# Moving a small MLP's VectorE work from between the key chunks to the ends of the key pairs, and looping its unrolled code, in a decode attention kernel

## The chip, the cores and the metric

The kernel runs on one core of one Trainium2 chip. The metric is the device time of a run in microseconds (us). A profile (one traced run) stands beside the timed runs. All traced runs were fast, and the comparisons use fast runs alone.

## The reference, cut to what matters

A decode step: one query token, 16 query heads over 8 key/value heads, a cache of 65,536 positions of 256 numbers for each. To its output a gated "mixer", a tiny MLP over the token axis, is added.

```python
q = (x @ wq) ...                                   # 16 heads of 256
scores = einsum("bhqd,bhkd->bhqk", q, k) * 256**-0.5
o = einsum("bhqk,bhkd->bhqd", softmax(scores), v)
a = o.reshape(...) @ wo
# the mixer: x is one row of 448; F = 1792 = 14 tiles of 128
h = layernorm(x);  u = gelu(einsum("bsd,sf->bdf", h, w1) + b1)
b = einsum("bdf,fs->bds", u, w2) + b2
out = g * a + (1 - g) * b                          # g: a sigmoid gate
```

The cache is 2 x 8 x 65,536 x 256 bf16 numbers, 537 MB. Each is used once, for two query heads.

## The kernel before

The cache is streamed in "pairs": 16,384 positions of K in two halves of 4 MB, then the same positions of V in one load of 8 MB. There are 32 pairs, four for each head. A K half is four "chunks". For each chunk TensorE transposes K into PSUM, VectorE and ScalarE each copy half of it to SBUF (the eviction), TensorE makes scores, ScalarE makes exponentials. After the eight chunks of a pair TensorE multiplies the weights with V.

The sync engine asks for the loads. There is room for one pair of K (two halves) and one of V, so each request waits for the work that frees its room:

```python
for j in range(NP):                      # 32 pairs, unrolled, one queue
    for a in range(2):
        if j >= 1:                       # the transposes that read this half are done
            eng.wait_ge(sem_tr[NB - 1], BODY * (j - 1) + DC * (a + 1))
        eng.dma_start(kring[:, a] ..., k_src(2 * j + a)).then_inc(sem_k[a], 16)
    ...
    else:
        eng.wait_ge(sem_pv, j)           # the values of the pair before are done
    ...
        eng.dma_start(vbuf ..., v_src(j)).then_inc(sem_v, 16)
```

The mixer has 14 tiles of 128 x 448. A tile is seven small VectorE operations (part A), a tanh on ScalarE, three more VectorE operations (part B). In the kernel before, VectorE's code for the whole first head is unrolled, 32 chunks, with part A of one tile and part B of another behind an eviction; ScalarE's first three pairs are unrolled too. From then on both run loops.

```python
on = OrderedEngineSet([vec.engine])
for c in range(NCPH):                    # the 32 chunks of the first head, unrolled
    evacuate(c % BODY, c)
    if 0 <= c - B0 - 2 < FT:
        b_partB(c - B0 - 2)
    if 0 <= c - B0 < FT:
        b_partA(c - B0)
finish_head(0)
with nc.Fori(1, H - 1, 1, engines=on) as g:
    with nc.Fori(0, PPH, 1, engines=on) as m:
        ...
        for k in range(BODY):
            evacuate(k, c0 + k)
    finish_head(g)
```

The softmax here doesn't subtract the row's maximum and nothing guards it: scores larger than these inputs give would overflow.

## Time and profile before

| | before |
|---|---|
| median of the first three runs | 1273.26 us (1272.3 to 1273.73) |
| span of the traced run | 1270.2 us |
| cache traffic | 544.22 MB read from HBM |
| VectorE / ScalarE busy | 33% / 42% of the span |

From the page of the kernel before: busy time, the DMA row of the 40 slices, the queues, and the chain that ended last.

```profile
PE 944.5 (74%) x16936; PEld 861.9 (68%) x16936; DVE 415.7 (33%) x727; ACT 535.4 (42%) x786; POOL 0.9 (0%) x7
DMA  9999999999999999999999999999999999999998
...
q1 hardware_dynamic: 16866, 544.22, 99.6%
q8 instruction: 8, 0.13, 0.0%
q14 instruction: 6, 0.05, 0.0%
...
DMA 73%; PE 21%; DVE 3%; issue 1%; ACT 1%; DVEq 0%; SPq 0%
```

The load queue (q1) is busy 99.6% of the span, and loads make up most of the chain.

A stretch of the timeline of the first head (start, duration, engine, operation; in brackets how long the engine had waited and for whom):

```profile
71.32 3.33 PE L257 MATMUL kst<-ident,kring 128*128 128x128 f32 x16 [2.27 <-DVE ktT L492]
71.96 0.28 DVE L482 TENSOR_SCALAR zring<-zring 128x448 bf16<-128x448 bf16 x1
...
75.76 0.28 DVE L475 TENSOR_SCALAR zring<-zring 128x448 bf16<-128x448 bf16 x1
75.95 1.28 DVE L492 COPY ktT<-kst 128x1024 bf16<-128x1024 bf16 x2
76.69 1.97 PE L257 MATMUL kst<-ident,kring 128*128 128x128 f32 x16 [1.23 <-DVE ktT L492]
```

Between two evictions (L492) VectorE works through a tile for some 4 us, and TensorE's transposes (L257) wait for it. The next chunk comes 5.4 us after this one; without mixer work a chunk takes 2.59 us.

What the sync engine asked for, and when (its timeline from 60 to 145 us; "x2" with a long duration is the two K halves merged: the second request starts 0.33 us before the end of it):

```profile
64.33 0.33 SPq L218 DMA_DIRECT2D vbuf<-in_A_v_cache_dram  x1
78.69 21.03 SPq L211 DMA_DIRECT2D kring<-in_A_k_cache_dram  x2
110.36 0.33 SPq L218 DMA_DIRECT2D vbuf<-in_A_v_cache_dram  x1
125.18 12.46 SPq L211 DMA_DIRECT2D kring<-in_A_k_cache_dram  x2
142.98 0.33 SPq L218 DMA_DIRECT2D vbuf<-in_A_v_cache_dram  x1
```

One line of the list of waits (us in total, times, longest), the stretch that holds the first head's stalls (its columns: stretch, its length, busy time of PE, PEld, DVE, ACT and POOL, granted clock, DMA share, GB/s), and three V loads from the chain (start is the request, start plus duration the landing on the slowest of the DMA engines):

```profile
PE kst L257 <- DVE ktT L492: 17.0, 10, 2.4
...
20.00:140.00 120.00, 91.45 (x1460) 84.74 (x1464) 76.48 (x188) 56.93 (x86) 0.00 (x0) 0.84 0.99 424
...
142.98 27.98 DMA vbuf<-in_A_v_cache_dram
176.22 34.13 DMA vbuf<-in_A_v_cache_dram
1076.63 32.84 DMA vbuf<-in_A_v_cache_dram
```

These are V of pairs 3, 4 and 27 (counted from 0). They landed at 170.96, 210.35 and 1109.47 us. In steady stretches a pair's loads take 38.8 us at 432 to 433 GB/s. The Trainium skill, "DMA: Bandwidth & Descriptors", Specifications, gives 435 GB/s as the ceiling of the fabric; the trace agrees within 1%.

### The profile page before, as it was taken

What the parts mean: (1) busy time and instruction counts of PE and PEld (TensorE: products, weight loads), DVE (VectorE), ACT (ScalarE), POOL (GpSimd) and SP (SyncE); (2) the same over time, 40 slices, a digit from 0 to 9 for tenths busy, and PEclk for the clock granted to TensorE, in tenths of its full rate; (3) what the DMA queues carried; (4) which work ended last, traced back from release to release, by engine and by line L of the source; (5) the groups of instructions that cost most, each with busy time, mean ns of one, the idle gap of its engine ahead of it and who ended that gap; (6) DMA issues with size and microseconds to landing.
All of it is one profiled execution on the core that took longest, in us unless ns stands there. A gap on an engine that the chain in (4) does not pass through costs nothing.

```text
span 1270.2 us, 37440 instructions
## 1 busy us (share of the span) xinstructions
PE 944.5 (74%) x16936; PEld 861.9 (68%) x16936; DVE 415.7 (33%) x727; ACT 535.4 (42%) x786; POOL 0.9 (0%) x7
## 2 busy tenths in 40 slices
PE   3878966877767787577875787856878677896668
PEld 3767965777657776567765677756778566776668
DVE  2786422332223333123331233312333222342223
ACT  1554633553334544245532355423454233553335
POOL 0000000000000000000000000000000000000000
PEclk9887987887878878788887889877888778897879
DMA  9999999999999999999999999999999999999998
GB/s 411 422 429 426 429 429 419 433 448 429 431 419 437 429 445 431 419 437 429 445 431 429 426 429 445 431 431 423 429 431 446 431 423 429 431 446 431 438 415 349
DMA packets 16892, 544.41 MB, mean 429 GB/s; under 512 B 1768, under 2 KB 3819, under 8 KB 4206
## 3 DMA queue, kind: packets, MB, share of 16 engines
q1 hardware_dynamic: 16866, 544.22, 99.6%
q8 instruction: 8, 0.13, 0.0%
q14 instruction: 6, 0.05, 0.0%
q10 hardware_dynamic: 12, 0.01, 0.0%
HBM read 544.22 MB, written 0.00 MB: 428 GB/s over the span
## 4 chain that ended last, share of the span: by engine, by line
DMA 73%; PE 21%; DVE 3%; issue 1%; ACT 1%; DVEq 0%; SPq 0%
DMA vbuf<-in_A_v_cache_dram 65%; PE acc L296 13%; DMA kring<-in_A_k_cache_dram 8%; PE kst L257 6%; PE sps L269 2%; ACT zring L578 0%; DVE ktT L492 0%; DVE wtmp L467 0%; DVE zring L469 0%; DVE zring L473 0%; DVE uring L465 0%; DVE wtmp L463 0%; DVE gu L485 0%; PE acc L390 0%; DVE wtmp L471 0%
## 5 line engine op out<-in xcount | busy, mean ns | idle before, releaser
L592 ACT ACTIVATE ktT<-kst 128x1024 bf16<-128x1024 bf16 x512 | 498.7, 1021 | 693.3 <-PE kst L257 693.0
L257 PE MATMUL kst<-ident,kring 128*128 128x128 f32 x4096 | 553.7, 296 | 128.6 <-DMA kring<-in_A_k_cache_dram 101.5
L257 PEld LDWEIGHTS kst<-ident,kring 128*128 128x128 f32 x4096 | 502.2, 153 | 141.1 <-issue 121.8
L492 DVE COPY ktT<-kst 128x1024 bf16<-128x1024 bf16 x512 | 352.9, 691 | 725.2 <-PE kst L257 702.7
L296 PE MATMUL acc<-vbuf,pT 128*2 128x256 bf16 x4064 | 178.1, 357 | 168.1 <-DMA vbuf<-in_A_v_cache_dram 167.5
L296 PEld LDWEIGHTS acc<-vbuf,pT 128*2 128x2 bf16 x4064 | 116.5, 108 | 223.1 <-DMA vbuf<-in_A_v_cache_dram 170.2
L269 PEld LDWEIGHTS sps<-qcur,ktT 128*128 128x128 bf16 x8192 | 239.0, 97 | 6.5 <-DVE ktT L492 3.5
L269 PE MATMUL sps<-qcur,ktT 128*128 128x2 bf16 x8192 | 237.6, 163 | 3.4 <-DVE ktT L492 3.3
L582 ACT ACTIVATE pT<-sps 128x32 bf16<-128x32 f32 x256 | 51.8, 202 | 13.4 <-PE sps L269 13.4
L497 DVE COPY accs<-acc 128x288 f32<-128x288 f32 x8 | 3.7, 458 | 97.0 <-PE acc L296 97.0
L287 PE MATMUL acc<-pT,ones_sq 128*128 128x32 bf16 x256 | 16.4, 178 | 4.0 <-issue 0.9
L287 PEld LDWEIGHTS acc<-pT,ones_sq 128*128 128x128 bf16 x256 | 10.9, 96 | 7.2 <-ACT pT L582 6.2
L578 ACT ACTIVATE zring<-zring 128x448 bf16<-128x448 bf16 x14 | 8.1, 578 | 7.4 <-DVE zring L475 7.4
L329 PE MATMUL prj<-wo_sb,oTn 128*1 128x448 bf16 x32 | 7.3, 351 | 3.2 <-DVE oTn L508 3.2
L346 PE MATMUL acc<-ones_sq,gu 1*128 1x1 bf16 x42 | 1.3, 161 | 8.4 <-DMA b_b<-in_B_b_dram 8.4
L346 PEld LDWEIGHTS acc<-ones_sq,gu 1*128 1x128 bf16 x42 | 1.2, 99 | 8.5 <-DMA b_b<-in_B_b_dram 8.5
L322 PE MATMUL acc<-zrow,ones_sq 1*128 1x292 bf16 x9 | 2.8, 310 | 4.7 <-DVE accs L497 4.0
L329 PEld LDWEIGHTS prj<-wo_sb,oTn 128*1 128x1 bf16 x32 | 2.2, 81 | 5.3 <-issue 3.6
L485 DVE TENSOR_TENSOR gu<-wtmp,zring 128x448 bf16<-128x448 bf16 x14 | 5.5, 392 | 1.1
L467 DVE TENSOR_TENSOR wtmp<-uring 128x448 bf16<-128x448 bf16 x14 | 5.5, 393 | 1.0
L469 DVE TENSOR_TENSOR zring<-wtmp,uring 128x448 bf16<-128x448 bf16 x14 | 5.5, 392 | 1.0
L473 DVE TENSOR_TENSOR zring<-uring,wtmp 128x448 bf16<-128x448 bf16 x14 | 5.5, 392 | 1.0
(79 smaller groups left out, 78.3 us busy)
## 6 DMA issues: line engine op xcount, KB each, us to landing
kring<-in_A_k_cache_dram SPq DMA_DIRECT2D x64, 4096.0 KB, 27.6
vbuf<-in_A_v_cache_dram SPq DMA_DIRECT2D x1, 4096.0 KB, 22.9
wo_sb<-in_A_wo_dram SPq DMA_DIRECT2D x8, 448.0 KB, 31.9
vbuf<-in_A_wq_dram SPq DMA_DIRECT2D x1, 3072.0 KB, 10.2
vbuf<-in_A_v_cache_dram SPq DMA_DIRECT2D x1, 2048.0 KB, 27.4
vbuf<-in_A_v_cache_dram SPq DMA_DIRECT2D x1, 1024.0 KB, 29.4
vbuf<-in_A_v_cache_dram SPq DMA_DIRECT2D x2, 512.0 KB, 30.6
vbuf<-in_A_wq_dram SPq DMA_DIRECT2D x1, 512.0 KB, 11.0
```

Source lines behind the costliest of these rows:

```text
L257: ins = pe.transpose(kst[:, b, j * P:(j + 1) * P], kring_f[:, a, r * NT + 4 * b + j, :], ident[:, :])
L269: ins = pe.matmul(sps[:, par, 2 * nt:2 * nt + 2], ktT[:, par, b, ntl * DH + dj:(ntl + 1) * DH:2], qcur[:, dj, :], start=(dj == 0), stop=(d ...
L287: pe.matmul(acc[:, DENC:SELC], ones_sq[:, :], pT[:, r, :], start=False, stop=(r == BODY - 1), skip_group_check=True)
L296: ins = pe.matmul(acc[o:o + REP, 0:DH], pT[:, r, 2 * nt:2 * nt + 2], vbuf[:, n, :], start=False, stop=False, skip_group_check=True)
L329: ins = pe.matmul(prj[0:1, 0:DM], oTn[:, j:j + 1], wo_sb[:, hh, dj * DM:(dj + 1) * DM], start=False, stop=True, skip_group_check=True)
L467: vec.tensor_tensor(W, U, U, op=ALU.mult)
L469: vec.tensor_tensor(Z, W, U, op=ALU.mult)
L473: vec.tensor_tensor(Z, U, W, op=ALU.add)
L492: vec.tensor_copy(ktT[:, k % KTB, b, :], kst_b[:, b, :]).then_inc(sem_ev[b], 1)
L578: act.activation(zring[:, slot, :], zring[:, slot, :], AF.Tanh).then_inc(s_tanh, 1)
L582: act.activation(pT[:, k, :], sps[:, k % 2, 0:2 * NT], AF.Exp, scale=scale).then_inc(sem_exp, 1)
L592: act.activation(ktT[:, k % KTB, b, :], kst_b[:, b, :], AF.Copy).then_inc(sem_ev[b], 1)
```

## The change

The intent: VectorE idles for some 17 us at the end of every K pair, until the next K lands. Put the mixer there: two tiles at a time, as one block, at the ends of the first seven pairs. As the block is then the same in every pair, VectorE and ScalarE each need only one loop, with a branch round the block. The core of the diff, with cuts:

```diff
-            for c in range(NCPH):
-                evacuate(c % BODY, c)
-                if 0 <= c - B0 - 2 < FT:
-                    b_partB(c - B0 - 2)
-                if 0 <= c - B0 < FT:
-                    b_partA(c - B0)
-            finish_head(0)
-            with nc.Fori(1, H - 1, 1, engines=on) as g:
+            with nc.Fori(0, H - 1, 1, engines=on) as g:
                 with nc.Fori(0, PPH, 1, engines=on) as m:
-                    c0 = vec.snap(g * NCPH + m * BODY, min_val=NCPH, max_val=NC)
+                    j = vec.snap(g * PPH + m, min_val=0, max_val=NP)
+                    c0 = vec.snap(j * BODY, min_val=0, max_val=NC)
                     for k in range(BODY):
                         evacuate(k, c0 + k)
+                    with vec.If(j < NMIX):
+                        mixer(j)
                 finish_head(g)
 ...
+            def mixer(j):                      # U, W, Z: 128 x 2 x 448
+                kt = vec.snap(kt_reg, min_val=0, max_val=FT - MT)
+                for i in range(MT):            # per-partition scalars: one tile at a time
+                    vec.tensor_scalar(wtmp[:, i, :], hbT[:, :], params[:, bass.ds(kt + i, 1)], None, op0=ALU.mult)
 ...                                            # the rest on both tiles at once
+                vec.tensor_scalar(Z, Z, GC0, None, op0=ALU.mult).then_inc(s_u, 1)
                 vec.tensor_scalar(W, U, 0.5, None, op0=ALU.mult)
+                vec.wait_ge(s_tanh, j + 1)
 ...
-            for c0 in range(0, HEAD, BODY):     # ScalarE
-                pair(c0, mix)
-            with nc.Fori(HEAD, NC, BODY, engines=OrderedEngineSet([act.engine])) as c0:
-                pair(c0)
+            with nc.Fori(0, NP, 1, engines=OrderedEngineSet([act.engine])) as j:
 ...
+                with act.If(j < NMIX):
+                    act.wait_ge(s_u, j + 1)
+                    act.activation(z_b[:, :, :], z_b[:, :, :], AF.Tanh).then_inc(s_tanh, 1)
```

## The prediction

> **What bounds the kernel.** The cache stream. The page gives the sync engine's DMA queue 99.6% of the span, 544.2 MB at 428 GB/s. The table of windows, cut at whole K/V pairs, shows 432 to 433 GB/s from 176 us to 1233 us; the Trainium skill ("DMA: Bandwidth & Descriptors", Specifications) puts the fabric ceiling at 435 GB/s, and this trace agrees. The chain of waits: DMA of V 65%, of K 8%, TensorE 21%.
>
> VectorE is busy 33%, ScalarE 42%. In a steady pair (timeline, 400 to 446 us) the K work takes some 22 us, one chunk per 2.59 us, paced by TensorE; then both engines idle about 17 us until the next K lands.
>
> **What the old mixer does.** In the first head a tile goes between every two chunks. In the timeline from 71 to 97 us chunks come 5.2 us apart where they stall (TensorE waiting 2.4 us on VectorE's eviction) instead of 2.6 us. The K part of pairs 0 to 2 takes about 31, 39 and 29 us, against 21 in pair 3. So V of pair 1 is asked for at 110.4 us and K of pair 3 at 125 and 137 us: just as the queue runs out.
>
> **What that costs now.** Little. The windows give 427, 423, 420 GB/s in 21-64, 64-110 and 110-143 us, against 432.5: 0.55 + 1.0 + 0.95, about 2.5 us. By landings in the chain: V of pair 3 lands at 170.96 us; start (3.2 us) + bytes at 432.5 GB/s + about 1.5 us of landing gives 169.5; V of pair 4 comes 39.4 us later where a plain pair takes 38.8. Sum 2.1 us. That is all the change can win.
>
> **The change.** Seven mixer blocks, each at the end of a K pair, in VectorE's gap. Durations today, 448 columns: two-tensor 0.39 us, immediate scalar 0.28, per-partition scalar 0.34. With about 0.16 us fixed (the smallest VectorE instructions take 0.14 to 0.17), 896 columns cost, by estimate, 0.63 and 0.39 us; the per-partition steps stay at 448, four of them. Block: 4 x 0.34 + 4 x 0.63 + 4 x 0.39 = 5.4 us, plus drains and a tanh of about 0.95 us, partly exposed: some 7 us. VectorE busy falls from 416 to about 407 us. It fits the 17 us gap, also in pair 0; the head's end waits for V anyway. ScalarE's wait and tanh fall into the same gap, after the last exponentials, so V is not held up. The branches cost some tenths of a us there. Tanh shares the table with exp (no reload in today's trace). The tail isn't touched.
>
> **Prediction.** 1271.3 us, 80% between 1268.5 and 1274.0; faster by over 2%: 1%, within 2%: 98%, slower by over 2%: 1%.
>
> **Right if:** the K part of pairs 0 to 2 takes 21 to 24 us, chunks come every 2.6 us, TensorE's waits on VectorE's eviction (17 us in total) nearly vanish, V of pair 1 is asked for near 97 us, GB/s of 21 to 143 us rises to about 432, V of pair 3 lands near 169 us, and later landings are 1 to 2 us earlier; mixer blocks take about 7 us.
>
> **Wrong if:** the early deficit isn't the queue running dry (gain 0); the block is longer than 17 us or ScalarE reloads tables round each branch and holds the exponentials; or the branches stall an engine every pair long enough to delay the loads' requests, which would cost 32 times.

## More of the kernel before

Queues 8 and 14 carry instructions: 14 packets, 0.18 MB.

One caution for what follows. The traced run of before took 1271.96 us, one of its fastest; over the calls its medians were 1273.19 to 1274.48 us, single runs 1271.81 to 1277.38.

## The result, and the profile after

Six runs of each kernel; of the kernel before, the first three are those above. The changed kernel took 1271.38 us (median; 1270.52 to 1272.23), the kernel before 1273.72 us (1272.3 to 1275.16). The ratio is 0.9982, with a 95% interval of 0.9969 to 0.9995: a gain of about 0.2%, within "same" at 2%. (Ratios are the mean time of one kernel's fast runs over that of the other's of the same rounds, so not quite the ratio of the medians.) Later it took 1271.54 us again.

The same lines after, first of the page:

```profile
PE 936.8 (74%) x16936; PEld 854.5 (67%) x16936; DVE 408.6 (32%) x671; ACT 534.4 (42%) x779; POOL 0.9 (0%) x7
...
q8 instruction: 8, 0.13, 0.0%
q14 instruction: 4, 0.02, 0.0%
...
DMA 81%; PE 18%; issue 0%; DVE 0%; ACTq 0%; DVEq 0%
```

VectorE's share of the chain has fallen from 3% to 0%. A block, in VectorE's timeline at the end of pair 0:

```profile
48.57 0.58 DVE L471 TENSOR_SCALAR wtmp<-hbT,params 128x448 bf16<-128x448 bf16 x2 [0.20 <-issue]
...
50.68 0.63 DVE L479 TENSOR_TENSOR z_b<-wtmp,u_b 128x896 bf16<-128x896 bf16 x1
51.39 0.39 DVE L481 TENSOR_SCALAR wtmp<-z_b 128x896 bf16<-128x896 bf16 x1
...
53.98 0.39 DVE L488 TENSOR_SCALAR z_b<-z_b 128x896 bf16<-128x896 bf16 x1 [0.72 <-ACT z_b L591]
54.54 0.63 DVE L490 TENSOR_TENSOR gu<-wtmp,z_b 128x896 bf16 x1 [0.17 <-issue]
```

It lasts from 48.57 to 55.17 us, 6.6 us; the next eviction comes at 64.56 us. TensorE's wait on VectorE's evictions has gone from the list of waits. The sync engine's requests, the same stretch, and the landings of V of pairs 3, 4 (169.82 and 208.60 us) and 27 (1107.68 us):

```profile
58.69 0.33 SPq L219 DMA_DIRECT2D vbuf<-in_A_v_cache_dram  x1
74.50 10.67 SPq L212 DMA_DIRECT2D kring<-in_A_k_cache_dram  x2
97.46 0.33 SPq L219 DMA_DIRECT2D vbuf<-in_A_v_cache_dram  x1
112.69 10.68 SPq L212 DMA_DIRECT2D kring<-in_A_k_cache_dram  x2
137.30 0.33 SPq L219 DMA_DIRECT2D vbuf<-in_A_v_cache_dram  x1
...
20.00:140.00 120.00, 86.66 (x1560) 79.51 (x1560) 48.67 (x84) 52.00 (x75) 0.00 (x0) 0.86 1.00 431
...
137.30 32.52 DMA vbuf<-in_A_v_cache_dram
175.47 33.13 DMA vbuf<-in_A_v_cache_dram
1073.89 33.79 DMA vbuf<-in_A_v_cache_dram
```

V of pair 2 is now asked for at 97 us instead of 110, the second K half of pair 2 at 85 instead of 99. The rate from 20 to 140 us rises from 424 to 431 GB/s, which over 120 us is about 2 us of loading. V of pair 27 lands 1.8 us earlier. That fits the prediction well. Does it prove its reason?

### The profile page after: what moved, and what is told of

It is laid out like the page before. It is cut to its first block, busy times and chain, and to the rows that moved or that the text cites. A ratio compares the mean times of both kernels' runs of the same rounds, so it can differ in the third digit from the quotient of the medians.

```text
span 1269.3 us, 37507 instructions
## 1 busy us (share of the span) xinstructions
PE 936.8 (74%) x16936; PEld 854.5 (67%) x16936; DVE 408.6 (32%) x671; ACT 534.4 (42%) x779; POOL 0.9 (0%) x7
## 4 chain that ended last, share of the span: by engine, by line
DMA 81%; PE 18%; issue 0%; DVE 0%; ACTq 0%; DVEq 0%
DMA vbuf<-in_A_v_cache_dram 74%; PE acc L297 13%; DMA kring<-in_A_k_cache_dram 7%; PE kst L258 3%; PE sps L270 1%; DMA b_b<-in_B_b_dram 1%; PE sps L359 0%; PE acc L391 0%; PE prj L330 0%; PE sps L311 0%; PE sps L361 0%; DVE out_b L556 0%; DVE xcb_row L544 0%; DVE stat L438 0%; ACTq L561 0%
## 5 line engine op out<-in xcount | busy, mean ns | idle before, releaser
L258 PE MATMUL kst<-ident,kring 128*128 128x128 f32 x4096 | 545.8, 293 | 127.3 <-DMA kring<-in_A_k_cache_dram 117.5
L258 PEld LDWEIGHTS kst<-ident,kring 128*128 128x128 f32 x4096 | 495.7, 152 | 138.8 <-issue 137.6
L591 ACT ACTIVATE z_b<-z_b 128x896 bf16<-128x896 bf16 x7 | 6.6, 950 | 21.0 <-DVE z_b L485 21.0
L490 DVE TENSOR_TENSOR gu<-wtmp,z_b 128x896 bf16 x7 | 4.4, 626 | 1.2 <-issue 1.2
L479 DVE TENSOR_TENSOR z_b<-wtmp,u_b 128x896 bf16<-128x896 bf16 x7 | 4.4, 626 | 0.5
L477 DVE TENSOR_TENSOR wtmp<-u_b 128x896 bf16<-128x896 bf16 x7 | 4.4, 625 | 0.5
```

Source lines behind the costliest of these rows:

```text
L258: ins = pe.transpose(kst[:, b, j * P:(j + 1) * P], kring_f[:, a, r * NT + 4 * b + j, :], ident[:, :])
L477: vec.tensor_tensor(W, U, U, op=ALU.mult)
L479: vec.tensor_tensor(Z, W, U, op=ALU.mult)
L490: vec.tensor_tensor(gu[:, bass.ds(kt, MT), :], W, Z, op=ALU.mult).then_inc(s_pb, 1)
L591: act.activation(z_b[:, :, :], z_b[:, :, :], AF.Tanh).then_inc(s_tanh, 1)
```

## The experiments

Theory A is the prediction's: the old place of the tiles made requests late, the load queue ran dry for some 2 us near 100 to 112 us, and the change takes that back. Rival B: the amount of VectorE work itself costs time. Rival C: the unrolled code costs. Later, Theory D was formed, see below. The diffs show the core of each edit; declarations and the counterparts on other engines are cut.

A load is split over 16 DMA engines and counts as landed only when the slowest has finished. The chain shows that one; the first engine's finish is read from the trace's semaphore counts. Both are in the table after the experiments.

### No mixer at all

The kernel before without its tiles. The result is wrong (relative error 0.92).

```diff
-                if 0 <= c - B0 - 2 < FT:
-                    b_partB(c - B0 - 2)
-                if 0 <= c - B0 < FT:
-                    b_partA(c - B0)
+            vec.memset(gu[:, :, :], 0.0).then_inc(s_pb, 1)     # once, ahead of the loop
```

> The kernel before with all fourteen mixer tiles left out (gu is filled with zeros once, so the result is wrong on purpose). Theory A, the queue ran dry because the old placement made requests late: V of pair 3 lands at 169.8 us and V of pair 4 at 208.6 us as in the changed kernel, against 170.96 and 210.35; the ratio to before is 0.998, no better than the change. Rival B, VectorE's amount of work itself costs time: clearly faster than the changed kernel, by some 1 to 3 us more. Rival C, the unrolled code costs: landings and time stay those of before.

1270.24 us (five runs, 1270.17 to 1271.04) beside 1274.09 us before, ratio 0.9970 (0.9954 to 0.9986). V of pair 3 landed at 170.18 us, of pair 4 at 208.99, of pair 27 at 1108.15. The landings are close to the changed kernel's. The time is 1.1 to 1.3 us below the changed kernel's medians, though in other calls: some of what rival B asks for. The landings do not show where those come from (they are 0.5 us later, not earlier). The trace is no help: it is of the slowest of the five runs, 1271.04 us, and a traced run of the changed kernel took 1271.12 us. This was not settled.

### A tile in every second gap

Still unrolled, still between chunks, but spread over the whole first head:

```diff
-                if 0 <= c - B0 < FT:
-                    b_partA(c - B0)
+                i, odd = divmod(c - B0, 2)
+                if not odd and 0 <= i < FT:
+                    b_partA(i)                       # part B and the tanh likewise
```

> The kernel before with a mixer tile in every second gap between chunks, over 28 of the 32 chunks of the first head, still unrolled and still between chunks. Theory A: about four tiles of 2.6 us lengthen each of four K parts from 21 to some 31 us, which the queued requests cover, so V of pair 3 lands at 169.8 us and the ratio to before is 0.998. Rival: work between the chunks costs by itself (or the unrolled code does): V of pair 3 lands near 171 us and the ratio is 1.000.

1272.86 us (1272.36 to 1273.33) beside 1274.09; ratio 0.9989, interval 0.9973 to 1.0005. V of pairs 4 and 27:

```profile
175.16 35.11 DMA vbuf<-in_A_v_cache_dram
...
1076.41 33.03 DMA vbuf<-in_A_v_cache_dram
```

The first engine's landings are those of the changed kernel (206.30 us for V of pair 4), so the queue did not run dry, although TensorE still waited on VectorE. But the slowest engine landed V of pair 4 at 210.27 us and V of pair 27 at 1109.44 us, as late as in the kernel before. Taking away the dry spell in this way gave about half of the gain at the median, and its interval reaches from none of it to more than all.

### The blocks at the ends, but unrolled

The changed kernel with VectorE's first two heads and ScalarE's first seven pairs unrolled.

```diff
-            with nc.Fori(0, H - 1, 1, engines=on) as g:
+            for j in range(GU * PPH):                # GU = 2 heads
+                for k in range(BODY):
+                    evacuate(k, j * BODY + k)
+                if j < NMIX:
+                    mixer(j)
+                if j % PPH == PPH - 1:
+                    finish_head(j // PPH)
+            with nc.Fori(GU, H - 1, 1, engines=on) as g:
```

> The changed kernel with its blocks at the ends of the pairs, but VectorE's first two heads and ScalarE's first seven pairs unrolled instead of in one loop. Theory A: place alone decides, V of pair 3 lands at 169.8 us, ratio to before 0.998. Rival C, the loops (less code to fetch, no unrolled stretch) made the gain: V of pair 3 near 171 us, ratio 1.000.

> The kernel with the blocks at the ends but unrolled, once more, in one call with the others. Theory D (unrolled code needs more instruction fetches, each of which sets one DMA engine back): V of pair 6 and all later ones land 1 us or more behind the changed kernel's on the slowest engine (over 1 us after its 287.4 us), and the time is 1272.9 us as the first time, against 1271.4 to 1271.5 of the changed kernel in two calls. Theory A (place alone): 1271.5 us.

1272.88 us (1272.42 to 1273.56) and, the second time, 1273.03 us (1272.55 to 1273.24). The changed kernel's runs lie at 1270.5 to 1272.2: no run of one overlaps the other. But these were other calls, each on another chip, and before's median wandered between calls by 1.3 us; against before in their own calls the ratios are 0.9989 and 0.9987, beside 0.9982 twice. By these ratios the difference would be 0.6 to 0.9 us, by the medians 1.5 us: the times alone make a difference likely, no more. The traces are clearer. Of the second run, the instruction queue and V of pairs 3 and 27:

```profile
q14 instruction: 7, 0.06, 0.0%
...
137.20 32.63 DMA vbuf<-in_A_v_cache_dram
1076.41 33.17 DMA vbuf<-in_A_v_cache_dram
```

V of pair 3 lands at 169.83 us, exactly as in the changed kernel. V of pair 27 lands at 1109.58, 1.9 us later. (A looped kernel traced in the same call, the one with useless work in every chunk below, landed it at 1107.74, so the call is not the reason.) The delay comes after the mixer's first head, one step at a time. In the trace the first engine is never late (1105.80 us, as in the changed kernel); one engine falls behind, from 2.1 us after the first at pair 5 to 2.9 us at pair 6 (an instruction packet passes at 249 us) and 3.8 us at the end (another at 494 us).

The trace of the first of the two runs had shown the same (V of pair 27 at 1109.79) and had given Theory D: each fetch of instructions is served by one of the 16 DMA engines that carry the loads (the Trainium skill, "DMA: Bandwidth & Descriptors", Queues, rings and completion order, counts instruction refill among the uses of one queue row on the same 16 engines, each of which takes turns between its queues; in the trace it is q14). That engine falls behind, here by 0.7 and 0.9 us for the two packets named, and stays behind, since each load is cut into sixteen shares, and a load is done when its slowest share is.

### Seven tiles in each of two pairs, in looped code

Late requests without unrolled code, and many of them:

```diff
                     for k in range(BODY):
                         evacuate(k, c0 + k)
-                    with vec.If(j < NMIX):
-                        mixer(j)
+                        if k < PERP:                 # 7 single tiles
+                            with vec.If(j < NPK):    # pairs 0 and 1
+                                mixer(vec.snap(j * PERP + k, min_val=0, max_val=NP * PERP))
```

> The changed kernel's loops, but seven single tiles behind the first seven chunks of pairs 0 and 1 (fourteen in all), each waiting for its own tanh. Theory A: a chunk then takes about 5.8 us on VectorE instead of 2.6, the K parts of pairs 0 and 1 take 43 us, second K halves are asked for some 4 and 6 us after the queue went idle, and 6 to 16 us are lost: about 1283 us, all of it before 140 us of the run. Rival C (loops made the gain): no slower than the kernel before, 1271 to 1274 us.

1293.52 us (1290.53 to 1294.5), ratio 1.0147. More than expected, and rival C as the only cause falls. The sync engine's requests:

```profile
45.62 24.15 SPq L214 DMA_DIRECT2D kring<-in_A_k_cache_dram  x2
79.98 0.33 SPq L221 DMA_DIRECT2D vbuf<-in_A_v_cache_dram  x1
96.85 24.02 SPq L214 DMA_DIRECT2D kring<-in_A_k_cache_dram  x2
129.41 0.33 SPq L221 DMA_DIRECT2D vbuf<-in_A_v_cache_dram  x1
```

The second K halves of pairs 1 and 2 were asked for at the end of the first and third line, at 69.4 and 120.5 us. The K halves ahead of them had landed at 63.2 and 111.6 us, and nothing else was queued. V of pair 4 landed at 230.94 us instead of 208.60, which is 22.3 us, and the time is longer by 22 us. A real dry spell is paid more than in full: the queue stood empty for 6.3 and 8.9 us, 15.2 us in all. The rest is the start: the second K half of pair 1 landed 13.1 us after its request, where in a filled queue halves land 9.7 us apart. The expectation had left that out.

### The changed kernel again, and the dry spell alone in looped code

```diff
                     for k in range(BODY):
                         evacuate(k, c0 + k)
+                        with vec.If(j == 1):
+                            for _ in range(2):       # useless work, pair 1 alone
+                                vec.drain()
+                                vec.tensor_tensor(dum[:, 1, :], dum[:, 0, :], dum[:, 0, :], op=ALU.mult)
```

> The changed kernel unaltered, as the base that the others of this call are compared with. All theories: V of pair 3 lands at 169.8 us, V of pair 4 at 208.6 us, 1271.4 us.

> The changed kernel (loops, blocks at the ends) with some 3.6 us of useless VectorE work behind each chunk of pair 1 alone, so that its K part takes about 40 us and V of pair 2 is asked for near 110 us as in the kernel before: the dry spell of before, without its unrolled code. Theory A (the dry spell made the difference): V of pair 4 lands near 210.4 us, time as before, some 2 us above the changed kernel. Theory D (after the earlier runs: a load is done when its slowest DMA engine is; a short dry spell lets the slow engines catch up and so costs only part of its length; the rest of the difference was extra instruction fetches of unrolled code on single engines): first engine at 209 us, slowest at 209.7 us, 1 us or less above the changed kernel.

1271.54 and 1271.55 us. The dose (3072 columns) was too small: V of pair 4 came only 0.7 us later, and the time did not show it. It was repeated with 3248 columns:

> The dry spell in looped code, with a larger dose (some 3.8 us behind each chunk of pair 1), since the first dose put V of pair 4 only 0.6 us back on every engine. V of pair 2 should be asked for near 110.4 us as in the kernel before. Theory D: mean landing of V of pair 4 about 2 us back (209.5 us), the slowest only 0.6 to 1.2 us back (209.2 to 209.8), time 1 us or less above the changed kernel's 1271.5. Theory A: the slowest engine 1.8 us back (210.4 us), time 1273.3 us.

1273.62 us (1273.37 to 1275.58). The requests and V of pairs 3, 4 and 27:

```profile
78.69 20.04 SPq L213 DMA_DIRECT2D kring<-in_A_k_cache_dram  x2
109.22 0.33 SPq L220 DMA_DIRECT2D vbuf<-in_A_v_cache_dram  x1
...
140.68 31.54 DMA vbuf<-in_A_v_cache_dram
177.96 33.04 DMA vbuf<-in_A_v_cache_dram
1076.43 33.77 DMA vbuf<-in_A_v_cache_dram
```

The second K half is asked for at 98.4 us and V of pair 2 at 109.2 us, nearly as in the kernel before. V of pair 4 lands at 211.00 us, 2.4 us later than in the changed kernel, and the time is 2.1 us longer. The changed kernel and the smaller dose ran in another call, but the smaller dose is the same code but for the number of columns: V of pair 2 was asked for at 107.0 us there, 2.2 us earlier, and the time was 2.1 us shorter, so the added branches are not the reason. The dry spell alone, in looped code, costs what the prediction said for it. Theory D had expected the engines that lag to catch up during it and only 1 us to be lost; here they did not, and that part of D fell.

### Instructions that nobody needs

The changed kernel, with a long straight line of code on GpSimd, which has nothing else to do. The first try was void:

```diff
+            idle = eng.alloc_register("idle")
+            for _ in range(2000):
+                eng.reg_mov(idle, 1)
```

> The changed kernel with 2000 register moves in a straight line on the otherwise idle GpSimd, on nobody's path: only its instructions have to be fetched. Theory D: the page shows more instruction packets on queue 14; each sets one DMA engine back by about 0.5 us, so the slowest engine lags: V of pair 4 lands 1 to 8 us later than 208.6 and the run is 1 to 8 us longer than the changed kernel, though the bytes fetched are under 0.2 MB of 544. Theory A: nothing changes, 1271.4 us.

1271.73 us, and 37,507 instructions as in the changed kernel: the compiler had dropped the moves. It says nothing about the question. The second try used drains, which stay:

```diff
+            for _ in range(2000):
+                eng.drain()
```

> The changed kernel with 2000 drains in a straight line on the otherwise idle GpSimd (the register moves of the earlier try were dropped by the compiler: same 37507 instructions, no more fetches). 128 KB of code more to fetch, nothing on anyone's path. Theory D: more instruction packets on the page, and the slowest DMA engine lags by 0.3 to 0.6 us for each that falls on it: V of pair 4 lands 1 to 8 us after 208.6, the run is longer by about as much. Theory A: 1271.5 us.

1280.12 us (1279.19 to 1280.88), 8.6 us longer than the changed kernel, a little more than expected. The instruction queue and V of pairs 3 and 27:

```profile
q14 instruction: 19, 0.16, 0.0%
...
145.21 33.23 DMA vbuf<-in_A_v_cache_dram
1083.51 32.90 DMA vbuf<-in_A_v_cache_dram
```

Sixteen packets more than in the changed kernel's second trace (3), 8,192 bytes each, 0.13 MB out of 544, and V of pair 27 lands at 1116.41 instead of 1107.68 us. The first engine lands it at 1106.11, hardly later than in the changed kernel (1105.80), and fifteen of the sixteen stay within 2.2 us of each other. One is 10.8 us behind at pair 2, when the last of these packets is near, and still 10.3 us behind at pair 30. Per packet that is (10.8 - 2.1) / 16 = 0.54 us. The bytes, spread over all 16 engines, would take 0.3 us; on the one engine, at a sixteenth of 432.5 GB/s, 4.8 us by estimate. The trace has these packets at 0.31 us each for the most part, so some 0.2 us of each packet's delay stays unexplained.

### Useless VectorE work in every chunk

```diff
+                for _ in range(2):                   # in evacuate(), 1536 columns
+                    vec.drain()
+                    vec.tensor_tensor(dum[:, 1, :], dum[:, 0, :], dum[:, 0, :], op=ALU.mult)
```

> The changed kernel with two useless VectorE operations of about 1 us behind every chunk of all 32 pairs: a chunk then takes about 3.5 us on VectorE instead of TensorE's 2.6, a K part about 29 us instead of 22, VectorE is busy some 900 us instead of 409. Theories A and D: K part plus values stay under the 38.8 us that a pair's loads take, so nothing is late and the time is 1271 to 1273 us. Rival B (VectorE's work costs by its amount): clearly longer, by tens of us.

1275.13 us (1274.73 to 1275.55). The busy line of the page, and V of pair 27:

```profile
PE 971.3 (76%) x16936; PEld 872.1 (68%) x16936; DVE 859.4 (67%) x1184; ACT 534.6 (42%) x779; POOL 0.9 (0%) x7
...
1074.37 33.37 DMA vbuf<-in_A_v_cache_dram
```

VectorE does twice the work, 451 us more, and V of pair 27 lands at 1107.74 us, the same as in the changed kernel within 0.1 us. Not one load is late. The 3.6 us come from the last pair alone, where no load hides the work: its first K half lands at 1235.0 us in both kernels, and the span ends 34.4 us later in the changed kernel and 38.5 us later here. The expectation (1271 to 1273 us) had left the tail out. This limits rival B: work under the loads' shadow does not delay them, work in the tail costs.

### A try at a better version

The w2 row is loaded element by element in both kernels (1761 packets of 4 bytes); here it is one contiguous row.

```diff
-            act.dma_start(w2row_b[:, :], B_w2.rearrange("f a -> a f")).then_inc(sem_misc, 16)
+            act.dma_start(w2row_b[:, :], B_w2.rearrange("f a -> (f a)").rearrange("(o n) -> o n", o=1)).then_inc(sem_misc, 16)
```

> The changed kernel with the w2 row loaded as one contiguous row instead of element by element (1761 packets of 4 bytes at the start, 16 us of engine time, estimated 1 us over 16 engines). If the start is bound by the DMA engines: landings and time 0.5 to 1 us earlier, 1270.6 us. If not: the same as the changed kernel. All theories agree; it is a try at a better version.

1271.32 us beside 1271.54 for the changed kernel: no gain that the runs can tell. The first engine landed V of pair 27 0.3 us earlier (1105.47 us), the slowest not (1108.26 us). No version was found that clearly beats the changed kernel and computes the right result.

### The table

Landings of V loads in us in the traced runs; times are medians of all runs of a label. "Dry" means that requests came late in pairs 1 and 2.

```
kernel                    code      dry  pair 4 first / slowest   pair 27 slowest   q14   time us
before (a fast run)       unrolled  yes  209.12 / 210.35          1109.47            6    1273.19 to 1274.48
no mixer (wrong result)   unrolled  no   206.31 / 208.99          1108.15            4    1270.24
every second gap          unrolled  no   206.30 / 210.27          1109.44            8    1272.86
blocks, unrolled          unrolled  no   206.32 / 208.79          1109.79            7    1272.88
blocks, unrolled, again   unrolled  no   206.49 / 208.62          1109.58            7    1273.03
dry spell, first dose     looped    less 207.12 / 209.34          1108.53            4    1271.55
dry spell, second dose    looped    yes  208.67 / 211.00          1110.20            4    1273.62
changed                   looped    no   206.49 / 208.61          1107.68            4    1271.38
changed, again            looped    no   206.38 / 208.74          1107.91            3    1271.54
2000 drains on GpSimd     looped    no   206.50 / 217.25          1116.40           19    1280.12
work in every chunk       looped    no   206.53 / 208.63          1107.74            4    1275.13
```

The q14 counts are those of the page; in the first trace of "changed" and in "every second gap" one of them is a packet of 96 bytes.

Landings are not all of the time. From the last V landing to the end of the span the traced runs took 4.1 to 5.4 us (9.2 with work in every chunk), and this part was not explained. The traced run of before and that of every second gap landed the last V at 1266.05 and 1265.95 us and took 1271.96 and 1273.17 us: differences of about 1 us between single runs can lie there.

## Why the prediction was right or wrong

The time was right: 1271.3 us predicted, 1271.38 measured, and most of the signs it named came.

- *The cache stream bounds the kernel.* Right. The strongest proof is the run with 451 us of added VectorE work, in which no load was late.
- *The block takes some 7 us and fits the gap.* Right: 6.6 us. VectorE's busy time is 408.6 us (predicted 407). The two-tensor step at 896 columns took 0.63 us as estimated.
- *The K part of pairs 0 to 2 takes 21 to 24 us, TensorE's waits on VectorE vanish, V is asked for near 97 us.* Right: 23.3, 23.3 and 22.7 us; 97.46 us. (Counted from 0, as the prediction counts elsewhere, the load that it calls V of pair 1 is V of pair 2.)
- *V of pair 3 lands near 169 us, later ones 1 to 2 us earlier.* The first is 169.82, so 0.8 us off; later ones are 1.75 us earlier (pair 4) and 1.8 us (pair 27).
- *GB/s of 21 to 143 us rises to about 432.* Nearly: 431 from 20 to 140 us. But the three windows from which the prediction summed 2.5 us show 426, 437 and 425 GB/s in the changed kernel: in the first nothing was gained, though 0.55 us of loss had been counted there.
- *The dry spell costs about 2.1 us.* Right in size: put back into looped code it set V of pair 4 back by 2.4 us and the time by 2.1 us (against the changed kernel). How the 2.1 us were found was partly luck. 0.6 us of them stood for V of pair 4 coming 39.4 us after V of pair 3 and not 38.8. That was no dry spell: in the trace of before the first fifteen landings of the two loads are 38.8 to 38.9 us apart and only the last 39.4, with an instruction packet at 199 us between. Nor did K of pair 3, asked for at 125 and 137 us, come late: each half landed 9.7 us after the load ahead of it, as in a filled queue.
- *"That is all the change can win."* This step failed. The prediction saw the loops only as a small cost ("The branches cost some tenths of a us there"). In fact the unrolled code cost something by itself, with no dry spell at all: V of pair 27 landed 1.7 to 2.1 us later in two traces against two of the changed kernel, and the medians differ by 1.5 us (between calls). With the dry spell alone removed (tiles in every second gap) the kernel gained 1.2 us at the median, and the interval reaches no gain. At the medians, the whole gain needs both parts.

The sum came out because the two costs do not add: 2.1 + 1.5 would be 3.6 us, and the kernel before is 2.3 us slower than the changed one. The trace of before hints at why. There the slowest engine was 2.3 us behind the first at pair 1 and only 0.6 us behind at pair 2, after the dry spell: engines that lagged caught up while the others had nothing to do. So against the changed kernel V of pair 3 came 2.6 us later on the first engine but only 1.1 us on the slowest; the packet at 199 us then added 0.6 us on the slowest, which makes the 1.7 us of pair 4. With seven tiles in each of two pairs the lag shrank in the same way, from 2.2 us at pair 0 to 0.7 us at pair 1. But in the looped dry spell the slowest stayed 2.3 us behind, and why is not known. So this explanation fits two traces and fails in a third; it is argued, not shown. Open as well is why the kernel without a mixer ran at 1270.24 us, and why the kernel before scatters more (1271.8 to 1277.4 us) than any other here.

That instruction fetches hold up single DMA engines was shown by adding fetches and nothing else on the path: sixteen packets, 8.6 us, one lagging engine. That the unrolled kernel's 1.5 us come from its own three or four extra packets is inferred from their times in the trace, of which two match the steps of the lagging engine, and from the size of the steps, 0.7 and 0.9 us.

## What to carry to other kernels

In a kernel bound by its loads, ask of any compute only whether it delays a request until the queue is dry, and how much of it lies in the tail after the last load; under those limits VectorE's load could double without delaying one load. A load that is split over 16 DMA engines is as slow as the slowest engine: look at the spread of the landings and not only at GB/s, because a few stray packets on one engine (here instruction fetches, 0.5 to 0.9 us each) delay everything after them. And when a change moves the place of work and also the form of the code, test each alone: the sum was right here, and half of the reason was missing.

## What the Trainium skill lacked or had wrong

- "Runtime: NRT & Kernel Launch", Instruction fetch mechanics, calls the cost of crossing an instruction block "mostly hidden" and says that kernels "prefer full unrolling where possible". Whatever the fetches cost the engine that ran the code, which was not measured, they were not hidden for the loads: sixteen extra fetches on an idle engine cost 8.6 us, 0.54 us each, and the unrolled form was about 1.5 us slower than the looped one at the medians, between calls. The DMA page puts refills on the same 16 engines as the loads but names no cost.
- The same section speaks of refills in blocks of 16 KiB. The sixteen extra fetches moved 0.13 MB, 8,192 bytes each in the trace; only queue 8's packets had 16,384 bytes.
- "DMA: Bandwidth & Descriptors", Why a DMA increments its semaphore by 16 and not by 1, says that the engines finish independently and only the full 16 means that all has landed. The traces agree, and add sizes: first and slowest engine are 2.1 us apart in the changed kernel, and a lag of 10.8 us at pair 2 was still 10.3 us 28 pairs later, so a steady queue does not even it out.
- "VectorE: DVE Perf Modes", the walkthrough of the modes, holds: two bf16 results per cycle (the same page, Specifications, gives 0.96 GHz) make 448 columns 0.233 us by estimate, and the two-tensor step grew from 0.393 to 0.626 us between 448 and 896 columns.
